# A job's output copied to SBUF by ScalarE, its sums and low parts formed on VectorE during the next job's value products

## The chip, the cores and the metric

The kernel runs on one core of a Trainium2 chip. A core has five engines with a queue of instructions each: TensorE (PE in the profile; its weight loads are shown apart as PEld), VectorE (DVE), ScalarE (ACT), GpSimd (POOL) and SyncE (SP), which here only issues DMAs. Each engine works through its own queue in order; semaphores hold an instruction until what it needs is there. The metric is the device time of one execution in microseconds (us); lower is better.

## The reference

What is computed, cut to what matters:

```python
# q, k, v: (2 batches, 8 heads, 576 positions, 64)
psi_rel = log1p(abs(i - j)); psi_i = log1p(max(i, 1))
bias    = relu((psi_rel / psi_i)[..., None] @ w1 + b1) @ w2        # 32 hidden units, 8 heads
attn    = softmax(q @ k.T / 8 + bias)                               # over 576 positions
x       = (attn @ v) laid out as (1152 tokens, 512)
x       = (silu(x @ w_gate) * (x @ w_val)) @ w_out                  # 512 -> 1536 -> 512
out     = softplus(x @ w_in) @ w_out2                               # 512 -> 2048 -> 512
```

All inputs are float32 (the weights of the two last lines float64).

## The kernel before

**Stages.** From 0 to about 60 us the position bias is computed. From there to about 188 us attention runs, and from 188 us to the end the two feed-forward layers, one long row of matmuls (lines 722, 673 and 1030).

**Units, jobs and slots.** Attention has eight units (a pair of heads of one batch each, in the order of `UNITS`, line 477). A unit has two jobs, `sub` 0 with 256 query rows per head and `sub` 1 with 320. I write job (4,1) for unit 4, sub 1. A job is cut into 4 or 5 chunks of scores, and `run_slot` (line 493) treats one chunk per slot, nine slots to a unit. The order in which a slot writes out its instructions is the order of every engine's queue in this stage (`manual_schedule` names all engines): scores on PE (`ps<-kst,ql` and `ps<-kst,qh`, line 326); `finish` of the job whose value products have just ended; copies of transposed blocks out of PSUM (`at<-pt`, mostly ACT, one piece on DVE); bias and row minimum on DVE (`e,sm<-ps,bias`, line 347); the exponential of the chunk before on ACT, its reciprocal on DVE and the scaling on POOL (line 369); two steps of preparing the next unit's keys and queries; the steps of jobs in `late`; transposes on PE (`pt<-ident,e`); and, in one slot of a job, all its value products on PE (`po<-at,v`, line 423) in one go.

**High and low parts.** An operand in float32 is split into a rounded high part and the rest (`kst`, `qh` and `ql`, `B11h` and `B11l`), so that three fast products give a precise one. Line 189 forms the rest for keys and queries, mostly on POOL, line 443 (the helper `minus`) for the outputs.

**What becomes of an output.** The first feed-forward layer is computed with seven products instead of eight: the output is cut into four quarters, units 0 and 2 giving B11, units 1 and 3 B12, units 4 and 5 B22, units 6 and 7 B21. Besides B11, B21 and B22 it wants the sums T1 = B12 - B11, T2 = B22 - T1, T3 = B22 - B12 and T4 = B21 - T2, each as high and low part. `finish` (line 433) forms all that from `po`, the one PSUM bank of value products. It is a generator: each `yield` hands the rest to the next slot. VectorE reads `po` two or three times in the slots that follow the job (`t2f<-po,bias`, `t<-po,bias`, `B22l<-po,B22h`); POOL forms the low parts of T2, T3 and mostly T4; ACT rounds the high parts.

**Buffers.** Two PSUM buffers hold scores (`psS`), three hold transposed blocks (`psT`), one holds `po`. A score can be written when the DVE instruction that read its buffer two scores earlier is done. `t` is one SBUF tile for T3 and T4 on their way to POOL.

Of the kernel before, what the change touches and what calls it, by code (L numbers as in the profile page):

```python
# [40 lines left out]
PLAIN = 2  # L41

WARM = 12


KHIGH, KLOW = "va", "ppvp"
# [54 lines left out]
def tile_kernel(ctx: ExitStack, tc, qT, kT, vS, vT, wb, wg, wv, wo, wi, wo2, table, out):  # L101
# [25 lines left out]
    with ExitStack() as actx:  # L127
# [303 lines left out]
        def finish(u):  # L431

            if u["i"] == 2 and u["sub"] == 0:
                slots(xp, "a", ("B21", "B22"))
            if u["i"] == 4 and u["sub"] == 0:
                right.close()
                SLOTS["rp8"] = (None, opener(rctx)("rp8", 1, side="right"))
                slots(SLOTS["rp8"][1], "r", ("T2", "T3", "T4"))
            pr, sub, po = u["pr"], u["sub"], u["po"]
            n = 320 if sub else 256  # L440
            cols = slice(256 * sub, 256 * sub + n)
            po = po[:, :n]
            minus = lambda o, a, b, eng=nc.vector: eng.tensor_tensor(o, a, b, op=ALU.subtract)
            at = lambda name: [t[:, pr % 2, cols] for t in SLOTS[name][1]]
            floats = lambda name: [t.bitcast(F32) for t in at(name)]
            name = f"B{1 + pr // 2}{1 + u['b']}"
            if name != "B12":
                nc.scalar.copy(at(name)[0], po)
            k = pr % 2
            home = bias[1][:, 2 * k : 2 * k + 2, cols]  # L450
            t1f, b12 = home[:, 0], home[:, 1]
            chains = []
            if name == "B12":
                nc.scalar.copy(b12, po)
                minus(t1f, po, floats("B11")[0])
                minus(t1f, t1f, floats("B11")[1])
                chains = [("T1", t1f)]
            elif name == "B22":
                t2, t3 = t2f[:, k, cols], tmpp.tile([P, 320], F32, name="t")[:, :n]
                minus(t2, po, t1f)  # L460
                minus(t3, po, b12)
                chains = [("T2", t2), ("T3", t3)]
            elif name == "B21":
                t4 = tmpp.tile([P, 320], F32, name="t")[:, :n]
                minus(t4, po, t2f[:, k, cols])
                chains = [("T4", t4)]
            if not u["eager"]:
                yield
            if name != "B12":
                minus(at(name)[1], po, floats(name)[0])  # L470
            if u["eager"]:
                yield
                yield
            for to, t in chains:
                nc.scalar.copy(at(to)[0], t)
                yield
                minus(at(to)[1], t, floats(to)[0], nc.vector if to == "T1" or u["eager"] else nc.gpsimd)

        UNITS = [(0, 0), (0, 1), (1, 0), (1, 1), (2, 1), (3, 1), (2, 0), (3, 0)]

# [8 lines left out]
        prep = iter(())  # L489
        before = None  # L490
        slot = 0

        def run_slot():
            nonlocal turned, done, prep, before, slot
# [28 lines left out]
                u = units[i][sub]  # L523
                got = scores(u, n)
            for w in done:
                w["eager"] = slot >= len(chunks) - 1
                late.append(finish(w))
                if w["eager"]:
                    next(late[-1])
# [7 lines left out]
                before = None  # L537
            for _ in range(2):
                next(prep, None)
            late[:] = [steps for steps in late if next(steps, late) is not late]  # L540
            held, turned = [t[:2] for t in turned], []

            over = slot >= len(chunks)
# [8 lines left out]
            for _ in range(len(gathered) if last_job else max(ends, default=0)):  # L552
                w, piece = gathered.pop(0)
                values(w, piece)
                if piece == PIECES[w["sub"]][-1]:
                    done.append(w)
            if slot < len(chunks):
                before = (u, n)
                if n == 3 + sub:
# [4 lines left out]
        with tc.manual_schedule(engines={E.PE, E.Activation, E.DVE, E.Pool, E.SP}):  # L564
# [26 lines left out]
            fp = pool("fp", 1)  # L591
            psT = pool("psT", 3, space=PSUM)
            psO = pool("psO", 1, space=PSUM)
            while slot < len(chunks) or jobs or turned or gathered or done or late:
                run_slot()


# [525 lines left out]
```

## Time and profile before

| | |
|---|---|
| median of 3 runs | 589.54 us (589.43 to 589.64) |
| the profiled execution's own time | 589.42 us |
| its span, first to last instruction | 587.6 us |
| PE busy | 579.3 us, 99% |
| PEld busy | 509.9 us, 87% |
| DVE busy | 452.9 us, 77% |
| ACT busy | 374.1 us, 64% |
| POOL busy | 98.9 us, 17% (nearly all of it between 50 and 181 us) |
| granted TensorE clock | 0.999 |

A busy PE in this table is not PE at its peak, since matmuls overlap and their ends are modelled. What PE loses in attention is better read from the weight loads (PEld): the idle time that a load shows in brackets, and what ended it.

### The profile page before, as it was taken

Reading aid. Unit: us, or ns where it says so; the run is one execution under the profiler, and the core shown is the slowest. Engines: PE = TensorE matmul, PEld = TensorE weight load, DVE = VectorE, ACT = ScalarE, POOL = GpSimd, SP = SyncE. Lnnn points to the kernel's source line nnn. Section 1 sums busy time; section 2 is a strip of 40 time slices with the busy share of each in tenths; the row PEclk is TensorE's granted clock in tenths of the full one; section 3 lists DMA queues with packets and bytes.
Section 4 is the critical chain, followed back from the end, with each engine's and each line's share of the span. In section 5 each row is a group of like instructions: output and inputs, shape, how many; then the busy total and the mean of one; then the engine's idle time right before and its main releaser. Section 6 shows DMA issues by size and latency. Waiting matters only on the chain.

```text
span 587.6 us, 11306 instructions
## 1 busy us (share of the span) xinstructions
PE 579.3 (99%) x4274; PEld 509.9 (87%) x4274; DVE 452.9 (77%) x972; ACT 374.1 (64%) x711; POOL 98.9 (17%) x147
## 2 busy tenths in 40 slices
PE   8999999999999999999999999999999999999997
PEld 6444578888887999999999999999989989989986
DVE  6999778788888998987879626579998876974432
ACT  6999887888888866755567425359736725733520
POOL 0002578888971000000000000000000000000000
PEclk9999999999999999999999999999999999999999
DMA  8999623333233342232344231222343241310012
GB/s 316 208 205 211 160 74 111 112 112 100 82 111 103 114 131 84 91 126 73 84 139 139 71 97 53 105 85 76 92 158 127 73 143 29 117 36 1 2 59 102
DMA packets 42038, 63.30 MB, mean 108 GB/s; under 512 B 4224, under 2 KB 30848, under 8 KB 41984
## 3 DMA queue, kind: packets, MB, share of 16 engines
q1 hardware_dynamic: 41840, 62.57, 36.4%
q8 instruction: 33, 0.54, 0.4%
q14 instruction: 21, 0.17, 0.1%
q10 hardware_dynamic: 144, 0.02, 0.0%
HBM read 49.60 MB, written 2.36 MB: 88 GB/s over the span
## 4 chain that ended last, share of the span: by engine, by line
PE 85%; DVE 7%; ACT 4%; POOL 2%; DMA 1%; issue 1%; POOLq 0%; DVEq 0%; ACTq 0%
PE pw L722 38%; PE pw L1030 17%; PE pw L673 13%; PE po L423 6%; PE ps L326 4%; PE pt L396 3%; PE pb L263 2%; ACT early L275 2%; ACT r L253 2%; DVE e L347 2%; PE ps L299 1%; DVE r L255 1%; DMA bias<-early 1%; PE warm L567 1%; DVE bias L347 1%
## 5 line engine op out<-in xcount | busy, mean ns | idle before, releaser
L1030 PE MATMUL pw<-oh,g2h 128*128 128x512 f32 x144 | 56.2, 390 | 0.0
L1030 PE MATMUL pw<-oh,g2l 128*128 128x512 f32 x144 | 56.2, 390 | 0.0
L1030 PE MATMUL pw<-ol,g2h 128*128 128x512 f32 x144 | 56.1, 390 | 0.0
L673 PE MATMUL pw<-gl,sh 128*128 128x384 f32 x144 | 48.2, 335 | 0.0
L673 PE MATMUL pw<-gh,sl 128*128 128x384 f32 x144 | 48.2, 334 | 0.0
L673 PE MATMUL pw<-gh,sh 128*128 128x384 f32 x144 | 48.2, 334 | 0.0
L255 DVE TENSOR_SCALAR r<-G 128x576 f32<-128x576 f32 x108 | 47.2, 514 | 0.0
L263 PE MATMUL pb<-r,wb_sb 128*32 128x288 f32 x576 | 46.7, 412 | 0.3 <-DVE r L255 0.2
L647 DVE SCALAR_TENSOR_TENSOR x<-raw,x 128x512 int32<-128x512 int32 x68 | 46.2, 687 | 0.9
L369 POOL TENSOR_SCALAR e<-e,sm 128x576 f32<-128x576 f32 x44 | 34.5, 795 | 66.3 <-DVE sm L366 58.9
L263 PEld LDWEIGHTS pb<-r,wb_sb 128*32 128x32 f32 x576 | 21.6, 109 | 24.4 <-DVE r L255 9.0
L347 DVE CUSTOM_DVE_ANT_0 e<-ps,bias 128x576 f32<-128x576 f32 x44 | 33.0, 749 | 12.4 <-PE ps L326 7.6
L403 ACT COPY at<-pt 128x512 f32<-128x512 f32 (+2 forms) x69 | 36.4, 547 | 6.0 <-PE pt L396 5.5
L326 PE MATMUL ps<-kst,ql 128*128 128x288 f32 x120 | 37.1, 338 | 1.4 <-DVE sm L347 0.7
L423 PE MATMUL po<-at,v 128*64 128x256 f32 (+3 forms) x384 | 36.8, 332 | 1.0 <-DVE at L403 0.8
L1068 DVE TENSOR_TENSOR acc<-pw,acc 128x512 f32<-128x512 f32 x27 | 17.5, 684 | 25.1 <-PE pw L1030 25.1
L361 ACT ACTIVATE e<-e,sm 128x576 f32<-128x576 f32 x44 | 34.3, 780 | 3.0 <-DVE sm L347 1.9
L644 DVE TENSOR_SCALAR x<-x 128x512 int32<-128x512 int32 x68 | 28.7, 427 | 9.3 <-ACT x L643 5.1
L423 PEld LDWEIGHTS po<-at,v 128*64 128x64 f32 x384 | 26.7, 137 | 8.2 <-issue 1.5
L1030 PEld LDWEIGHTS pw<-oh,g2l 128*128 128x128 f32 x144 | 27.0, 188 | 5.8
L326 PE MATMUL ps<-kst,qh 128*128 128x288 f32 x120 | 32.0, 295 | 0.0
L396 PE MATMUL pt<-ident,e 128*128 128x128 f32 x188 | 31.6, 276 | 0.1
(269 smaller groups left out, 1659.6 us busy)
## 6 DMA issues: line engine op xcount, KB each, us to landing
raw<-in_wo_dram SPq DMA_DIRECT2D x28, 512.0 KB, 3.5
bias<-early SPq DMA_DIRECT2D x32, 288.0 KB, 7.2
raw<-in_wi_dram SPq DMA_DIRECT2D x16, 512.0 KB, 4.0
raw<-in_wv_dram SPq DMA_DIRECT2D x12, 512.0 KB, 4.5
raw<-in_wg_dram SPq DMA_DIRECT2D x12, 512.0 KB, 3.6
qr<-in_qT_dram SPq DMA_DIRECT2D x7, 576.0 KB, 3.7
bias<-in_kT_dram SPq DMA_DIRECT2D x6, 576.0 KB, 4.4
v<-in_vS_dram SPq DMA_DIRECT2D x8, 384.0 KB, 3.3
```

Source lines behind the costliest of these rows:

```text
L255: nc.vector.tensor_scalar(r, G[:, w0 : w0 + S], PB[:, n : n + 1], 0.0, op0=ALU.add, op1=ALU.max)
L263: nc.tensor.matmul(pb[32 * ct : 32 * ct + 32, hf, :HALF], W2, rs[ct][:, HALF * hf : HALF * (hf + 1)], start=True, stop=True,)
L326: nc.tensor.matmul(ps[:, hf, :HALF], u[t][:, o : o + P], kst[:, a, HALF * hf : HALF * (hf + 1)], start=i == 0, stop=i == len(parts) - 1,)
L347: nc.vector.tensor_tensor_reduce(out=e[:, :S].rearrange("p (a n) -> p a n", a=2), in0=ps[:, :, :HALF], in1=bt.rearrange("p (a n) -> p a n" ...
L369: nc.gpsimd.tensor_scalar(e, e, sm[:, 3, i : i + 1], 1.0, op0=ALU.mult, op1=ALU.mult)
L396: nc.tensor.transpose(pt[:, P * w : P * (w + 1)], e, ident)
L403: marks[eng, u["i"], u["sub"]] = copy(at[:, :w], pt[:, :w]).ins
L423: nc.tensor.matmul(u["po"][D * a : D * (a + 1), o : o + n], v[:, D * t : D * (t + 1)], at[:, i : i + n], start=piece == 0 and o == 0, stop ...
L647: nc.vector.scalar_tensor_tensor(yi, lw, 29, yi, op0=ALU.logical_shift_right, op1=ALU.bitwise_or)
L673: nc.tensor.matmul(ps[:, :n], w[:, k], x, start=first and k == 0 and i == 0, stop=last and k == NK - 1 and i == 2)
L722: nc.tensor.matmul(ps[:, hf, :HALF], a[:, o + k], b[:, HALF * hf : HALF * (hf + 1)], start=start and k == 0 and i == 0, stop=k == 1 and i ...
L1030: nc.tensor.matmul(ps, g, w.rearrange("p k f -> p (k f)"), start=f == 0 and i == 0, stop=f == 3 and i == 2)
```

## The change

ACT now copies the output of a B22 or B21 job from `po` to SBUF at once (into `t` for sub 1; for sub 0 into `over`, the spare last columns of `bias4`). The subtractions then take the SBUF copy in place of `po`. The generator says `BLOCK` where it has to wait for the next job's value products: `advance` puts it into the list `waiting`, and `run_slot` goes on with that list right behind a job's value products. B11 is as before, B12's sum T1 and its low part wait in the same way, and the last job (7,1) still reads `po`.

```diff
+            over = bias[4][:, :2].rearrange("p a s -> p (a s)")[:, 5 * P :]
+            room = lambda: (tmpp.tile([P, 320], F32, name="t") if sub else over)[:, :n]
             if name == "B12":
                 nc.scalar.copy(b12, po)
-                minus(t1f, po, floats("B11")[0])
+                yield BLOCK
+                minus(t1f, b12, floats("B11")[0])
                 minus(t1f, t1f, floats("B11")[1])
-                chains = [("T1", t1f)]
-            elif name == "B22":
-                t2, t3 = t2f[:, k, cols], tmpp.tile([P, 320], F32, name="t")[:, :n]
-                minus(t2, po, t1f)
-                minus(t3, po, b12)
-                chains = [("T2", t2), ("T3", t3)]
-            elif name == "B21":
-                t4 = tmpp.tile([P, 320], F32, name="t")[:, :n]
-                minus(t4, po, t2f[:, k, cols])
-                chains = [("T4", t4)]
-            if not u["eager"]:
                 yield
-            if name != "B12":
+                nc.scalar.copy(at("T1")[0], t1f)
+                yield BLOCK
+                minus(at("T1")[1], t1f, floats("T1")[0])
+                return
...
+            t = room()
+            if u["i"] == 2 * NP - 1 and sub:
+                minus(t, po, t2f[:, k, cols])
+                minus(at(name)[1], po, floats(name)[0])
                 yield
+            else:
+                nc.scalar.copy(t, po)
+                yield BLOCK if u["i"] < 7 else None
+                minus(at(name)[1], t, floats(name)[0])
+                if name == "B22":
+                    minus(t2f[:, k, cols], t, t1f)
+                    chains = [("T2", t2f[:, k, cols])]
+                minus(t, t, b12 if name == "B22" else t2f[:, k, cols])
                 yield
+            chains.append(("T3" if name == "B22" else "T4", t))
             for to, t in chains:
                 nc.scalar.copy(at(to)[0], t)
                 yield
-                minus(at(to)[1], t, floats(to)[0], nc.vector if to == "T1" or u["eager"] else nc.gpsimd)
+                minus(at(to)[1], t, floats(to)[0], nc.vector if u["eager"] else nc.gpsimd)
...
-                w["eager"] = slot >= len(chunks) - 1
+                w["eager"] = slot >= len(chunks)
...
-            late[:] = [steps for steps in late if next(steps, late) is not late]
+            advance(late)
...
+            if done:
+                advance(waiting)
```

PE's and SP's queues are word for word the same; what moves stands on DVE, ACT and POOL.

**DVE, from the end of job (4,0) to the end of job (4,1).** Before (`bias_85` is the tile with the mixed chunk, `bias_83` and `bias_84` hold chunks, `bias_72` the next keys, `bias_73` b12 and t1f):

```order
L443 TENSOR_TENSOR t2f<-po,bias_73 128x256
L443 TENSOR_TENSOR t<-po,bias_73 128x256
L347 ISA bias_83,sm<-ps,bias_83 128x576
...
L185 CAST kst<-bias_72 128x576
L443 TENSOR_TENSOR B22l<-po,B22h 128x256
L347 ISA bias_83,sm<-ps,bias_83 128x576
...
L185 CAST qh<-qr 128x256
L347 ISA bias_84,sm<-ps,bias_84 128x576
```

After, the same stretch ends so, with the value products of (4,1) on PE beside it:

```order
L349 ISA bias_84,sm<-ps,bias_84 128x576
L349 ISA sm 128x1
L187 CAST qh<-qr 128x256
L445 TENSOR_TENSOR T1l<-bias_73,T1h 128x320
L445 TENSOR_TENSOR B22l<-bias_85,B22h 128x256
L445 TENSOR_TENSOR t2f<-bias_85,bias_73 128x256
L445 TENSOR_TENSOR bias_85<-bias_85,bias_73 128x256
L349 ISA bias_84,sm<-ps,bias_84 128x576
```

The three subtractions of (4,0) have left the places between its next chunks and stand, with a fourth that is left from (3,1), in one piece ahead of the first chunk behind the value products; none of them reads `po` any more.

**POOL, while unit 5 prepares its sub 1 and the keys of the unit after.** Before:

```order
L189 TENSOR_TENSOR ql<-qr,qh 128x320
L443 TENSOR_TENSOR T2l<-t2f,T2h 128x320
L443 TENSOR_TENSOR T3l<-t,T3h 128x320
L369 TENSOR_SCALAR e_104<-e_104,sm 128x576
L369 TENSOR_SCALAR e_105<-e_105,sm 128x576 x2
L189 TENSOR_TENSOR kst<-bias_72,kst 64x288 x3
L443 TENSOR_TENSOR T2l<-t2f,T2h 128x256
L369 TENSOR_SCALAR bias_83<-bias_83,sm 128x576 x2
L189 TENSOR_TENSOR ql<-qr,qh 128x256
L443 TENSOR_TENSOR T3l<-t,T3h 128x256
L189 TENSOR_TENSOR ql<-qr,qh 128x256
```

After:

```order
L445 TENSOR_TENSOR T2l<-t2f,T2h 128x256
L371 TENSOR_SCALAR e_104<-e_104,sm 128x576
L191 TENSOR_TENSOR ql<-qr,qh 128x320
L445 TENSOR_TENSOR T3l<-bias_85,T3h 128x256
L371 TENSOR_SCALAR e_104<-e_104,sm 128x576
L371 TENSOR_SCALAR e_105<-e_105,sm 128x576 x2
L191 TENSOR_TENSOR kst<-bias_72,kst 64x288 x2
L445 TENSOR_TENSOR T2l<-t2f,T2h 128x320
L191 TENSOR_TENSOR kst<-bias_72,kst 64x288
L445 TENSOR_TENSOR T3l<-t,T3h 128x320
L371 TENSOR_SCALAR bias_83<-bias_83,sm 128x576 x2
L191 TENSOR_TENSOR ql<-qr,qh 128x256 x2
```

T3l no longer stands between the two 256-wide `ql`; the low parts of one job now come about one job later, T2l ahead of the second 320-wide `ql` and among the keys.

**ACT, around the end of job (5,0).** Before:

```order
L448 CAST B22h<-po 128x256
L403 COPY at<-pt 128x512
L361 ACTIVATE e_105,sm<-e_105,sm 128x576
L475 CAST T2h<-t2f 128x256
L403 COPY at<-pt 128x512 x2
```

After:

```order
L487 CAST T2h<-t2f 128x320
L450 CAST B22h<-po 128x256
L477 COPY bias_85<-po 128x256
L405 COPY at<-pt 128x512
L363 ACTIVATE e_105,sm<-e_105,sm 128x576
L487 CAST T3h<-t 128x320
L405 COPY at<-pt 128x512 x2
```

One copy is added, and it writes where POOL's T3l of the job (4,0) still reads, so it waits for POOL; T2h, now of the job before, stands ahead of it.

## Rows read from the trace of the kernel before

**Rows 1.** Timeline, PEld, 78 to 130 us: start, us, instruction, idle before and releaser.
```profile
78.43 0.19 PEld L326 LDWEIGHTS ps<-kst,ql 128*128 128x128 f32 x1 [0.34 <-POOL ql L189]
80.62 0.19 PEld L326 LDWEIGHTS ps<-kst,ql 128*128 128x128 f32 x1 [0.32 <-DVE sm L347]
...
89.89 0.19 PEld L326 LDWEIGHTS ps<-kst,ql 128*128 128x128 f32 x1 [0.30 <-DVE sm L347]
...
94.08 0.19 PEld L326 LDWEIGHTS ps<-kst,ql 128*128 128x128 f32 x1 [0.39 <-issue]
...
97.96 0.19 PEld L326 LDWEIGHTS ps<-kst,ql 128*128 128x128 f32 x1 [0.73 <-DVE sm L347]
...
120.95 0.30 PEld L326 LDWEIGHTS ps<-kst,ql 128*128 128x128 f32 x2 [0.43 <-DVE sm L347]
...
128.40 0.19 PEld L326 LDWEIGHTS ps<-kst,ql 128*128 128x128 f32 x1 [0.36 <-POOL ql L189]
```

**Rows 2.** Timeline, PEld, 142 to 172 us.
```profile
145.63 0.19 PEld L326 LDWEIGHTS ps<-kst,ql 128*128 128x128 f32 x1 [0.40 <-POOL ql L189]
...
146.63 0.19 PEld L326 LDWEIGHTS ps<-kst,ql 128*128 128x128 f32 x1 [0.20 <-DVE sm L347]
...
153.76 0.30 PEld L326 LDWEIGHTS ps<-kst,ql 128*128 128x128 f32 x2 [0.29 <-DVE sm L347]
...
155.39 0.19 PEld L326 LDWEIGHTS ps<-kst,ql 128*128 128x128 f32 x1 [0.21 <-DVE sm L347]
...
162.29 0.19 PEld L326 LDWEIGHTS ps<-kst,ql 128*128 128x128 f32 x1 [0.31 <-POOL ql L189]
...
163.28 0.19 PEld L326 LDWEIGHTS ps<-kst,ql 128*128 128x128 f32 x1 [0.21 <-DVE sm L347]
...
170.40 0.30 PEld L326 LDWEIGHTS ps<-kst,ql 128*128 128x128 f32 x2 [0.28 <-DVE sm L347]
```

**Rows 3.** Timeline, PE, in the last jobs.
```profile
180.53 0.65 PE L423 MATMUL po<-at,v 128*64 128x256 f32 x4 [0.77 <-DVE at L403]
```

**Rows 4.** Two stretches: length, busy us of each engine, clock, DMA share, GB/s.
```profile
150.00:160.00 10.00, 9.95 (x92) 8.80 (x91) 8.06 (x24) 8.59 (x21) 9.33 (x13) 1.00 0.19 61
190.00:200.00 10.00, 10.00 (x78) 10.00 (x77) 8.98 (x21) 9.05 (x16) 0.00 (x0) 1.00 0.49 151
```

**Rows 5.** Line 443: count, ns min/median/max, first and last start, shapes.
```profile
L443 DVE TENSOR_TENSOR T1l<-bias,T1h x4: 404/552/908, 79.5 to 132.5; 128x256 fp32r<-128x256 f32 x2, 128x320 fp32r<-128x320 f32 x2
L443 DVE TENSOR_TENSOR t2f<-po,bias x4: 402/436/470, 135.5 to 161.7; 128x256 f32<-128x256 f32 x2, 128x320 f32<-128x320 f32 x2
```

**Rows 6.** Timeline, DVE and POOL, 122 to 125 us.
```profile
122.22 2.83 POOL L189 TENSOR_TENSOR kst<-bias,kst 64x288 fp32r<-64x288 f32 x3
...
123.00 0.46 DVE L189 TENSOR_TENSOR kst<-bias,kst 64x288 fp32r<-64x288 f32 x1 [0.81 <-ACT kst L183]
123.48 0.91 DVE L443 TENSOR_TENSOR T1l<-bias,T1h 128x256 fp32r<-128x256 f32 x1
```

**Rows 7.** Timeline, DVE, behind the value products of (4,1), (5,0) and (5,1).
```profile
140.89 0.70 DVE L365 TENSOR_SCALAR sm<-sm 128x2 f32<-128x2 f32 x1
...
143.63 0.76 DVE L347 CUSTOM_DVE_ANT_0 bias<-ps,bias 128x576 f32<-128x576 f32 x1 [0.75 <-PE ps L326]
...
150.93 0.76 DVE L347 CUSTOM_DVE_ANT_0 e<-ps,bias 128x576 f32<-128x576 f32 x1 [1.12 <-PE ps L326]
...
160.42 0.76 DVE L347 CUSTOM_DVE_ANT_0 bias<-ps,bias 128x576 f32<-128x576 f32 x1 [0.88 <-PE ps L326]
```

**Rows 8.** Timeline, POOL, 140 to 153 us.
```profile
140.84 0.73 POOL L443 TENSOR_TENSOR T2l<-t2f,T2h 128x256 fp32r<-128x256 f32 x1
...
144.15 0.74 POOL L443 TENSOR_TENSOR T3l<-t,T3h 128x256 fp32r<-128x256 f32 x1
...
151.69 0.89 POOL L443 TENSOR_TENSOR T3l<-t,T3h 128x320 fp32r<-128x320 f32 x1
```

**Rows 9.** Timeline, ACT, behind the value products of (5,0).
```profile
150.93 0.36 ACT L448 CAST B22h<-po 128x256 fp32r<-128x256 f32 x1
```

More of the change, by code (lines that the diff above doesn't have):

```diff
@@ L43 @@
 WARM = 12
+BLOCK = "block"
 KHIGH, KLOW = "va", "ppvp"
@@ L452, in finish @@
             chains = []
+            over = bias[4][:, :2].rearrange("p a s -> p (a s)")[:, 5 * P :]
+            room = lambda: (tmpp.tile([P, 320], F32, name="t") if sub else over)[:, :n]
             if name == "B12":
                 nc.scalar.copy(b12, po)
-                minus(t1f, po, floats("B11")[0])
+                yield BLOCK
+                minus(t1f, b12, floats("B11")[0])
                 minus(t1f, t1f, floats("B11")[1])
-                chains = [("T1", t1f)]
-            elif name == "B22":
-                t2, t3 = t2f[:, k, cols], tmpp.tile([P, 320], F32, name="t")[:, :n]
-                minus(t2, po, t1f)
-                minus(t3, po, b12)
-                chains = [("T2", t2), ("T3", t3)]
-            elif name == "B21":
-                t4 = tmpp.tile([P, 320], F32, name="t")[:, :n]
-                minus(t4, po, t2f[:, k, cols])
-                chains = [("T4", t4)]
-            if not u["eager"]:
-                yield
-            if name != "B12":
-                minus(at(name)[1], po, floats(name)[0])
-            if u["eager"]:
-                yield
+                yield
+                nc.scalar.copy(at("T1")[0], t1f)
+                yield BLOCK
+                minus(at("T1")[1], t1f, floats("T1")[0])
+                return
+            if name == "B11":
+                yield
+                minus(at(name)[1], po, floats(name)[0])
+                return
+            t = room()
+            if u["i"] == 2 * NP - 1 and sub:
+                minus(t, po, t2f[:, k, cols])
+                minus(at(name)[1], po, floats(name)[0])
+                yield
+            else:
[6 more added lines that the diff above has]
+                minus(t, t, b12 if name == "B22" else t2f[:, k, cols])
                 yield
+            chains.append(("T3" if name == "B22" else "T4", t))
             for to, t in chains:
@@ L491, in tile_kernel, with advance @@
         slot = 0
+        waiting, ended = [], object()
+        def advance(which):
+            steps_now, which[:] = which[:], []
+            for steps in steps_now:
+                said = next(steps, ended)
+                if said is BLOCK:
+                    waiting.append(steps)
+                elif said is None:
+                    late.append(steps)
         def run_slot():
@@ L593, in tile_kernel @@
             psO = pool("psO", 1, space=PSUM)
-            while slot < len(chunks) or jobs or turned or gathered or done or late:
+            while slot < len(chunks) or jobs or turned or gathered or done or late or waiting:
                 run_slot()
```

## The prediction

> **What bounds the kernel now.** I read the busy times by stretch first. From 190 us on PE is busy in every microsecond [rows 4], and the chain of waits runs through PE alone there; so whatever attention gains or loses arrives at the end whole. Inside attention PE looks busy too (9.95 of 10 us), but beside it POOL has 9.33, ACT 8.59 and DVE 8.06 [rows 4]: four engines near their limit, each feeding the others. What PE really loses is read next, from the weight loads ahead of the scores. Each load behind a value product shows 0.38 or 0.39 us of idle whichever engine is named, as at 94.08 [rows 1]; that is a pattern of its own, and I leave it out. What remains are six waits before 130 us (0.34 + 0.32 + 0.30 + 0.73 + 0.43 + 0.36 = 2.48 us [rows 1]), seven after it (0.40 + 0.20 + 0.29 + 0.21 + 0.31 + 0.21 + 0.28 = 1.90 us [rows 2]) and 0.77 us in the last jobs [rows 3]. That is 5.15 us, 0.9% of the kernel, and all that a change in attention can win. Nine of the thirteen name DVE's bias step and four POOL's `ql`; hence the third view, who stands ahead of those two on DVE and POOL.
>
> **The change part by part.** All sums go against the profiled execution's 589.42 us (587.6 us of span and 1.8 us around it); the median, 589.54, lies 0.12 above, and I add that at the end.
>
> *Waits that go.* The waits of 97.96, 120.95, 146.63, 153.76, 155.39, 163.28 and 170.40 each have one or two subtractions of line 443 just ahead of the bias step that PE waits for; that of 80.62 has T1l. These leave for the value products. 128.40 waits for a `ql` that is late because DVE spent 0.91 us on T1l [rows 6] ahead of it; 145.63 and 162.29 wait for a `ql` that has T3l (0.74 us [rows 8]) in front of it, which moves. 89.89 stands behind B11's low part, which stays, and 78.43 behind POOL's scaling: of its 0.34 I take 0.10. So before 130 us: 0.10 + 0.32 + 0.73 + 0.43 + 0.36 = 1.94 us; after: 1.90 us. What is late next are the copies and exponentials on ACT; the wait at 97.96 may keep half of its 0.73, since ACT's T1h now waits for the moved pair. In the last jobs the pair of subtractions (up to 0.47 us each [rows 5]) goes from ahead of the last bias step, but a copy and a waiting T4h join ACT: of 0.77 us [rows 3] I take 0.5, with 0 and 0.77 as bounds.
>
> *The added copies.* Seven copies out of PSUM on ACT, by the cast beside them 0.36 us for 256 columns [rows 9], by its width some 0.45 for 320: 2.8 us. They stand where ACT copies transposed blocks, of which PSUM holds three; T2h and T3h leave the same stretch at about the same price. I cost them at nothing; without that cover 0.36 us at a job's end, four to seven times, 1.4 to 2.5 us.
>
> *The subtractions in their new place.* The bias step behind the value products waits for PE's scores: 0.75, 1.12, 0.88 us of idle DVE [rows 7]. But 256 columns from PSUM cost 0.40 to 0.47 us whatever POOL does, while the same subtraction from SBUF costs 0.404 to 0.908 [rows 5], and the moved ones are now all of the second kind. Rows 6 show why: POOL is in three operations without a pause, DVE does one subtraction in 0.46 us, and the next, ready at once, takes 0.91, because a POOL operation went between. If they take turns like that, n subtractions cost n times 0.41 to 0.47 and a POOL operation of 0.73 to 0.89 us [rows 8] between any two, with about 0.4 for the one in progress.
>
> The Trainium skill ("SBUF — State Buffer", section "Who interferes with whom") says that a DVE instruction with two SBUF inputs contends with a GpSimd instruction that reads SBUF, one with at most one SBUF input does not, and that the loser blocks for the whole instruction. By that rule the trace agrees (0.470 at most against 0.908); if it did not hold, the sum below would lose its last term.
>
> What a place can hide: DVE's idle time, plus what the bias step may slip until PE needs its PSUM buffer two scores on. That slip is 145.63 - 0.40 - (143.63 + 0.76) = 0.84 us at (4,1) [rows 2, 7] and 162.29 - 0.31 - (160.42 + 0.76) = 0.80 at (5,1); for (5,0) and (6,0) I take 0.8 from these two.
> - (4,1): four subtractions, 0.47 + 3 x 0.41 = 1.70, and 0.4 + 2 x 0.74 for POOL, which then has nothing more ready: 3.6 us. Room 0.75 + 0.84 + 0.5 (the step of 0.70 us at 140.89 [rows 7] falls into T2l [rows 8], which leaves): 2.1. Over by 1.5.
> - (5,1): three, 1.23 + 0.4 + 2 x 0.74 = 3.1; room 0.88 + 0.80 = 1.7, since ACT's keys decide when DVE gets there. Over by 1.4.
> - (5,0) and (6,0): 3 x 0.47 + 0.4 + 2 x 0.89 = 3.6; room 1.12 + 0.8 and the 1.4 us of three subtractions that left: 3.3. Over by 0.3 each.
> - The places before have one to three subtractions and the room of T1l besides: nothing.
>
> That is 3.5 us if they always take turns, 0 if DVE keeps the port from one to the next. The pair of rows 6 takes turns, and I found no pair that does not; I take 3.3, near the upper end, for a turn now and then that finds POOL idle (0.67 of 10 us [rows 4]).
>
> Sum: -1.94 - 1.90 - 0.5 + 3.3 = -1.04 us, 588.4 in the profiled execution, 588.5 us as a median. Gain and price are both three to four times as large as what is left.
>
> **The rivals.**
> - *The cover is enough.* DVE runs its three or four in one piece, at most 0.4 us of waiting ahead: 1.6 to 2.1 us, which each room holds. For it: idle and slack are there in every place. Against it: rows 6. It gives -1.94 - 1.90 - 0.5 = -4.3; POOL, held 13 times for at most 0.41 us, has 0.67 of every 10 us free [rows 4], 2.3 in the 35 us that count, and could lose 5.3 - 2.3 = 3.0 us, of which a third is as much as PE would see: 585.2 to 586.2 us.
> - *Slower: POOL becomes the bound from (5,0) to (6,0).* A unit lasts 162.29 - 145.63 = 16.66 us there [rows 2], of which POOL is busy 93% [rows 4], some 15.5. Six subtractions that hold it for their whole 0.41 to 0.47 us add 2.6: 18.1, 1.5 us over, in two units. T2l now stands ahead of the second `ql`, and ACT's new copy may not overwrite `over` before T3l has read it: in the old trace a T3l ends at 152.58 [rows 8], the copy would stand at 151.29 [rows 9], and behind it the copies that PE needs: up to 1.3 us more. It decides from the point where the next unit's `ql` comes later than PE's scores by more than the 1.9 us won there. Price: 588.5 + 3.0 = 591.5, less if the stalls fall together: about 591. The rule of the Trainium skill ("SBUF — State Buffer", section "Who interferes with whom"), taken at its word, is this mechanism at its dearest. For it: POOL has next to no pauses; against it: T2l and T3l only moved, and PE's stalls give POOL time to catch up.
> - *Nothing comes of it.* The chain from scores over exponential, keys and `ql` to the next unit's scores runs over ACT; if that sets the unit's length, the stalls only change their names: 589.5 us.
>
> **How the numbers follow.** My forecast has 0.44, the cover 0.28, POOL as the bound 0.20, nothing 0.08. The predicted time is 588.5 us. The forecast's own range is 587.4 to 589.7; reaching into the first rival down to 585.4 and into the second up to 590.9 leaves about 2 in 10 out. A measurement of this kernel tells some 0.2% from no change, 1.2 us: below 588.36 is faster, above 590.72 slower. The forecast gives 0.22 to faster, 0.21 to same and 0.01 to slower; the first rival 0.28 to faster; the second 0.19 to slower and 0.01 to same; the third 0.08 to same. Together 0.50, 0.30, 0.20.
>
> **What would show it.** In the profile after: the waits before 130 us at 97.96, 120.95 and 128.40 are gone or small, and PE's first feed-forward matmul comes 1 to 2 us earlier than at 188. Taking turns shows as moved subtractions of 0.7 us and more with a POOL operation between, and as new PE waits for DVE's bias step two scores behind the value products of (4,1) and (5,1). If those subtractions stand 0.35 us apart, the first rival holds. If PE waits for `ql` at the start of units 6 and 7 by a microsecond, or ACT's copy names POOL's T3l, it is the second. I am wrong altogether if attention's length changes without a change in these PE waits, or if the feed-forward part gets PE waits of its own.

## The result and the profile after

The changed kernel takes 595.44 us (median of 4 runs, 595.24 to 596.30) against 589.52 (4 runs): ratio 1.0103, 95% interval 1.0086 to 1.0121. It is slower by 5.9 us, the other way from the forecast and outside the range. The profiled execution, the longest of the four, has a span of 594.3 us against 587.6. Times without a unit are in us.

Where the time went is read first from the start of each job's value products on TensorE:

| start of | before | after | after minus before |
|---|---|---|---|
| (2,0) | 99.13 | 98.04 | -1.09 |
| (4,0) | 131.39 | 129.68 | -1.71 |
| (4,1) | 139.75 | 138.58 | -1.17 |
| (5,0) | 147.79 | 148.32 | +0.53 |
| (6,0) | 164.44 | 168.30 | +3.86 |
| (6,1) | 172.95 | 177.31 | +4.36 |
| first feed-forward product | 188.12 | 193.69 | +5.57 |

Up to 130 us the change gives what was forecast. Between 130 and 194 us it loses 7.3. The weight loads with waits that answer to [rows 1] are down to these, beside those of 0.38 or 0.39 and a few of 0.3 or less elsewhere:

```profile
89.55 0.19 PEld L328 LDWEIGHTS ps<-kst,ql 128*128 128x128 f32 x1 [0.31 <-DVE sm L349]
...
105.38 0.19 PEld L328 LDWEIGHTS ps<-kst,ql 128*128 128x128 f32 x1 [0.28 <-DVE sm L349]
```

The matmuls that waited from 140 us on, in the kernel after (start, duration, instruction, idle before it and releaser). They answer to [rows 2, 3]:

```profile
144.09 0.40 PE L328 MATMUL ps<-kst,ql 128*128 128x288 f32 x1 [0.71 <-POOL ql L191]
146.02 0.37 PE L328 MATMUL ps<-kst,ql 128*128 128x288 f32 x1 [0.69 <-DVE sm L367]
154.28 0.66 PE L398 MATMUL pt<-ident,bias 128*128 128x128 f32 x4 [0.48 <-ACT at L405]
160.78 0.76 PE L425 MATMUL po<-at,v 128*64 128x128 f32 x5 [0.78 <-DVE at L405]
164.66 0.40 PE L328 MATMUL ps<-kst,ql 128*128 128x288 f32 x1 [0.65 <-POOL ql L191]
167.82 0.33 PE L398 MATMUL pt<-ident,bias 128*128 128x128 f32 x1 [0.36 <-POOL bias L371]
174.26 0.66 PE L398 MATMUL pt<-ident,bias 128*128 128x128 f32 x4 [0.47 <-ACT at L405]
...
185.31 0.65 PE L425 MATMUL po<-at,v 128*64 128x256 f32 x4 [1.08 <-DVE at L405]
189.10 1.29 PE L425 MATMUL po<-at,v 128*64 128x320 f32 x12 [0.81 <-ACT at L405]
196.11 0.50 PE L770 MATMUL pw<-B11h,wh 128*128 128x288 f32 x2 [0.57 <-DVE B21l L445]
```

They sum to 6.6 us, where PE before had 0.77 [rows 3] and two of 0.3 or less, and they name DVE, ACT and POOL: no single wait took the place of the old ones. What they have in common is seen in the row of subtractions behind (4,1)'s value products. The timeline of DVE, then of POOL, at the same time:

```profile
142.18 0.48 DVE L445 TENSOR_TENSOR T1l<-bias,T1h 128x320 fp32r<-128x320 f32 x1
142.57 0.88 DVE L445 TENSOR_TENSOR B22l<-bias,B22h 128x256 fp32r<-128x256 f32 x1
143.38 0.94 DVE L445 TENSOR_TENSOR t2f<-bias,bias 128x256 f32<-128x256 f32 x1
144.35 0.84 DVE L445 TENSOR_TENSOR bias<-bias,bias 128x256 f32<-128x256 f32 x1
145.12 0.74 DVE L349 CUSTOM_DVE_ANT_0 bias<-ps,bias 128x576 f32<-128x576 f32 x1
...
141.37 1.82 POOL L371 TENSOR_SCALAR bias<-bias,sm 128x576 f32<-128x576 f32 x2 [1.35 <-PE po L425]
143.16 1.76 POOL L191 TENSOR_TENSOR ql<-qr,qh 128x256 fp32r<-128x256 f32 x2
```

Four subtractions take 3.0 us here where they could take 1.8 (number 6 below), and the bias step behind them comes without DVE having idled (in [rows 7] it had 0.75). POOL pays as well: its two `ql` of 256 columns take 0.88 and 0.91 here, and one took 0.74 in the trace of before. The next unit shows how such lateness goes round. Rows of four engines, in order of time:

```profile
152.60 0.73 POOL L445 TENSOR_TENSOR T3l<-bias,T3h 128x256 fp32r<-128x256 f32 x1
...
153.37 0.37 ACT L477 COPY bias<-po 128x256 f32<-128x256 f32 x1 [1.37 <-POOL T3l L445]
...
155.02 0.15 DVE L367 TENSOR_SCALAR sm<-sm 128x1 f32<-128x1 f32 x1 [1.49 <-ACT e L363]
...
155.54 0.81 POOL L371 TENSOR_SCALAR e<-e,sm 128x576 f32<-128x576 f32 x1 [0.76 <-DVE sm L368]
...
157.67 2.33 DVE L191 TENSOR_TENSOR kst<-bias,kst 64x288 fp32r<-64x288 f32 x1 [1.26 <-ACT kst L185]
158.06 0.86 POOL L445 TENSOR_TENSOR T2l<-t2f,T2h 128x320 fp32r<-128x320 f32 x1
...
158.90 0.78 POOL L191 TENSOR_TENSOR kst<-bias,kst 64x288 fp32r<-64x288 f32 x1
...
160.03 0.69 DVE L405 COPY at<-pt 128x512 f32<-128x512 f32 x1
...
161.55 0.78 ACT L363 ACTIVATE m<-m,sm 128x576 f32<-128x576 f32 x1 [2.78 <-DVE sm L349]
```

ACT's new copy waits 1.37 us for POOL's T3l (the kernel before has no such copy), the exponential behind it is late, DVE waits 1.49 for that, POOL 0.76 for DVE. Then DVE's subtraction for the keys, which the change does not move, stands 2.33 us beside POOL's row (0.46 in [rows 6]); the copy behind it is what PE waits 0.78 us for at 160.78. Two stretches, 150 to 160 and 190 to 200 us, and the unit from (5,0) to (6,0):

```profile
150.00:160.00 10.00, 9.47 (x79) 7.53 (x75) 7.14 (x17) 7.40 (x20) 9.08 (x12) 1.00 0.19 61
190.00:200.00 10.00, 9.43 (x81) 8.20 (x77) 9.06 (x20) 7.66 (x16) 0.00 (x0) 1.00 0.32 93
...
148.32:168.30 19.98, 17.68 (x142) 14.05 (x141) 16.51 (x44) 15.00 (x39) 16.98 (x23) 1.00 0.17 53
```

Against [rows 4] DVE and ACT do less in ten microseconds while POOL is as busy as before, and the unit lasts 19.98 us instead of 16.65 (164.44 - 147.79; POOL was busy 15.50 of these).

### The profile page after: what moved, and what is told of

It reads as the page before. It is cut to its first block, busy times and chain, and to the rows that moved or that the text cites. A ratio compares the mean times of both kernels' runs of the same rounds, so it can differ in the third digit from the quotient of the medians.

```text
span 594.3 us, 11296 instructions
## 1 busy us (share of the span) xinstructions
PE 581.3 (98%) x4274; PEld 509.8 (86%) x4274; DVE 461.2 (78%) x971; ACT 375.1 (63%) x718; POOL 104.0 (17%) x148
## 4 chain that ended last, share of the span: by engine, by line
PE 77%; DVE 9%; ACT 8%; POOL 2%; DMA 1%; issue 1%; DVEq 0%; ACTq 0%; POOLq 0%
PE pw L748 37%; PE pw L1056 17%; PE pw L699 13%; PE po L425 3%; PE pt L398 2%; ACT early L277 2%; ACT r L255 2%; PE pb L265 2%; PE ps L328 2%; PE ps L301 1%; ACT at L405 1%; DVE r L257 1%; DMA bias<-early 1%; PE warm L593 1%; DVE e L349 1%
## 5 line engine op out<-in xcount | busy, mean ns | idle before, releaser
L371 POOL TENSOR_SCALAR e<-e,sm 128x576 f32<-128x576 f32 x44 | 35.8, 824 | 64.8 <-DVE sm L368 60.3
L425 PE MATMUL po<-at,v 128*64 128x256 f32 (+3 forms) x384 | 38.0, 333 | 2.7 <-DVE at L405 1.9
```

The costliest lines, as they stand in the source:

```text
L371: nc.gpsimd.tensor_scalar(e, e, sm[:, 3, i : i + 1], 1.0, op0=ALU.mult, op1=ALU.mult)
L425: nc.tensor.matmul(u["po"][D * a : D * (a + 1), o : o + n], v[:, D * t : D * (t + 1)], at[:, i : i + n], start=piece == 0 and o == 0, stop ...
```

## The experiments

The texts on record speak of these theories. A: the loss is made by subtractions with both operands in SBUF and POOL's instructions holding each other up. B: it begins with the B12 part. C: it is ACT's copy waiting for T3l. D: the last jobs lose by themselves. E: it is the new order and place. Ratios are to the kernel before on the same chip, with 95% intervals; differences in us are of medians, and the kernel before had 589.5 to 590.1 on these chips, so they are good to about half a microsecond.

**1. B12 alone.** The branches for B22 and B21, and the rule for the last jobs, are those of the kernel before.

> Only the B12 part of the change (jobs (2,0) to (3,1): copy to SBUF, sums and T1l where the next job's value products stand); B22 and B21 as in the kernel before. The first term of my sum was -1.9 for this, and the changed kernel is 1.7 us ahead at 129.68. Theory A (the loss is made by the moved B22 and B21 subtractions between 130 and 194 us, which take turns with POOL): 587.5 to 588.3. Theory B (the loss begins with B12, whose T1h copies on ScalarE now wait up to 2.2 us for VectorE and push what stands behind them): 589.3 or more.

589.80, ratio 1.0003 (0.9994 to 1.0012): inside B's range and not A's. But it is no slower than the kernel before either, so the 5.9 us come only with B22 and B21. It is 1.83 us ahead at (4,0), 1.09 at (4,1), and 0.13 behind at (5,0). So the B12 part does not make the loss, but its gain does not live either. The keys' subtraction of one unit earlier pays, beside three of POOL's (0.46 in the kernel before):

```profile
138.18 1.70 DVE L191 TENSOR_TENSOR kst<-bias,kst 64x288 fp32r<-64x288 f32 x1 [0.74 <-ACT kst L185]
```

**2. Two places for the copy.**
```diff
-            room = lambda: (tmpp.tile([P, 320], F32, name="t") if sub else over)[:, :n]
+            room = lambda: (tmpp.tile([P, 320], F32, name="t") if sub else over[:, 256 * (u["i"] % 2) :])[:, :n]
```


> The changed kernel, but the 256-column jobs copy their output by turns to two places instead of one, so that ScalarE's copies for (5,0) and (6,0) need not wait (1.37 us each) until POOL has read the place as T3. All else as in the changed kernel. Theory C (that wait, with the gather copies behind it, is most of the loss): 2.5 to 4 us less than the changed kernel, 591.5 to 593. Theory A (taking turns of VectorE and POOL): at most 1 us less, 594.4 to 595.5.

593.90, ratio 1.0066 (1.0049 to 1.0083). 1.5 us less than the changed kernel, between what C and A expected: without the wait a quarter of the loss is gone. That is more than the wait alone: in the profiled execution the keys' subtraction, now at 156.33, takes 0.71 instead of 2.33, and PE waits 1.25 us for `ql` at 162.62 and 1.35 for DVE at 165.21 instead.

**3. T2l to T4l on DVE.**
```diff
-                minus(at(to)[1], t, floats(to)[0], nc.vector if u["eager"] else nc.gpsimd)
+                minus(at(to)[1], t, floats(to)[0], nc.vector)
```


> The changed kernel, but the subtractions T2l, T3l and T4l run on VectorE, none on POOL, which keeps its key, query and scaling work. Theory A (POOL and VectorE in each other's way): POOL's seven low parts (0.5 to 0.9 us each) no longer stand in a row with the keys' subtraction, so VectorE's 2.33 us subtraction at 157.67 falls to about 1 us; VectorE gets some 5 us more work of its own, spread over 60 us: 593 to 594.5. Theory C (ScalarE waits for POOL's T3l): about the same, as T3l comes earlier on VectorE or not. If VectorE's own load is the bound: 597 or more.

592.44, ratio 1.0043 (1.0028 to 1.0058): 3.0 us less, more than A expected. The keys' subtraction that took 2.33 us takes 0.60. More work on DVE made the kernel faster; what stands on POOL counts.

**4. B21 as before.** The branch of the kernel before stands in for the four jobs from (6,0) on (with T4 of sub 0 in `over`).

> The changed kernel for B12 and B22; the four B21 jobs (6,0) to (7,1) as in the kernel before (the output read where it was accumulated, right after the copy; the rule for the last jobs as before). Theory D (the last jobs lose by themselves: VectorE's subtractions against POOL's scaling, copies on ScalarE, T4l on POOL): the 1.7 us between the start of (6,0)'s value products and the first product of the output projection come back, 593.2 to 594. Theory A: a little more, since (6,0)'s own subtractions no longer stand against POOL, 592.7 to 593.7. If the tail's loss was only carried over from before it: 595 to 595.5.

592.87, ratio 1.0049 (1.0034 to 1.0064), 2.6 us less: in A's range, below D's. From (6,0) to the first feed-forward product it needs 23.9 us, the changed kernel 25.4, the kernel before 23.7. So the last jobs lose 1.5 to 1.7 us by themselves. Behind that product the changed kernel loses 0.9 more against this run (400.6 us to the end of the span, and 399.7). What stands there in the changed kernel:

```profile
183.84 1.10 POOL L371 TENSOR_SCALAR bias<-bias,sm 128x576 f32<-128x576 f32 x1 [3.79 <-DVE sm L368]
...
185.17 0.82 DVE L445 TENSOR_TENSOR B21l<-t,B21h 128x320 fp32r<-128x320 f32 x1
...
187.83 0.37 ACT L477 COPY bias<-po 128x256 f32<-128x256 f32 x1 [0.99 <-POOL T4l L445]
...
195.59 0.46 ACT L487 CAST T4h<-t 128x320 fp32r<-128x320 f32 x1 [1.18 <-DVE t L445]
```

**5 and 6. POOL's work cut to an eighth, before and after.** In both kernels alike:
```diff
+            if by == "p" and i > 2:
+                l, h, src = (x[:, : x.shape[-1] // 8] for x in (l, h, src))
...
+                        e = e[:, : S // 8] if u["i"] > 2 else e
                         nc.gpsimd.tensor_scalar(e, e, sm[:, 3, i : i + 1], 1.0, op0=ALU.mult, op1=ALU.mult)
...
-                minus(at(to)[1], t, floats(to)[0], nc.vector if u["eager"] else nc.gpsimd)
+                c = n if to == "T1" or u["eager"] else n // 8
+                minus(at(to)[1][:, :c], t[:, :c], floats(to)[0][:, :c], nc.vector if u["eager"] else nc.gpsimd)
```


> The kernel before, with POOL's work of jobs 3 to 7 cut to an eighth of its columns: the lower parts of keys and queries, T2l to T4l and the scaling of the exponentials keep their places and their waits, but write only the first eighth (TensorE reads qh in place of ql, and the upper parts of T2 to T4 in place of the lower, so the values are not the reference's). It is the base for the next run. All theories: the waits for POOL go and VectorE is never held, 586 to 589.

> The changed kernel with the same cut of POOL's work to an eighth (same things left out as in the run before it). Theory A (the changed kernel loses because its SBUF subtractions and POOL's instructions hold each other up): with POOL's instructions short the loss is gone, and the time is below that of the kernel before with the same cut, by 1 to 4 us. Theory E (the loss comes from the order: subtractions late, more copies on ScalarE, VectorE's row of four in the window; POOL's long instructions have little part in it): still 3 us or more above the kernel before with the same cut.

587.07 (0.9952, 0.9937 to 0.9967) without the change and 584.75 (0.9911, 0.9895 to 0.9928) with it. TensorE reads `qh` in place of `ql` in both, so its waits for POOL's `ql` go too. With POOL out of the way the change wins 2.3 us; with POOL whole it loses 5.9. E is out: the order is the same in both. The four subtractions that took 3.0 us, here grouped by line (count, ns min/median/max):

```profile
L448 DVE TENSOR_TENSOR T1l<-bias,T1h x1: 478/478/478, 140.1 to 140.1; 128x320 fp32r<-128x320 f32 x1
L448 DVE TENSOR_TENSOR B22l<-bias,B22h x1: 471/471/471, 140.5 to 140.5; 128x256 fp32r<-128x256 f32 x1
L448 DVE TENSOR_TENSOR t2f<-bias,bias x1: 417/417/417, 140.9 to 140.9; 128x256 f32<-128x256 f32 x1
L448 DVE TENSOR_TENSOR bias<-bias,bias x1: 424/424/424, 141.3 to 141.3; 128x256 f32<-128x256 f32 x1
```

But the cut takes two things away at once: the holding up, and POOL's own lateness (T3l, `ql`, the scaling), so it does not size A alone.

**7. Not moved, from SBUF.**
```diff
-                yield BLOCK if u["i"] < 7 else None
+                yield
```


> The changed kernel, but the subtractions of B22 and B21 don't wait for the next job's value products: they follow ScalarE's copy by one slot, about where the kernel before has them, and read the SBUF copy. B12 as in the changed kernel. Theory A (SBUF operands against POOL, wherever they stand): the loss stays, 594 to 597. Theory E (the place is at fault: in the window they stand in a row of three or four ahead of the gather's copies and the exponentials' sums): most of the loss goes, 589.5 to 591.5.

600.14, ratio 1.0170 (1.0155 to 1.0186), 3.1 past A's range (594 to 597) and far from E's: the place in the window was the better one. That the SBUF operands are the trouble fits, but this run does not single them out, since ACT's copies stay and the three subtractions stand in another order than in the kernel before. Here the row stands ahead of a bias step for which PE waits. Timeline of DVE and PE, and a stretch:

```profile
137.04 0.88 DVE L445 TENSOR_TENSOR t2f<-bias,bias 128x256 f32<-128x256 f32 x1
137.96 0.90 DVE L445 TENSOR_TENSOR bias<-bias,bias 128x256 f32<-128x256 f32 x1
138.78 0.74 DVE L349 CUSTOM_DVE_ANT_0 bias<-ps,bias 128x576 f32<-128x576 f32 x1
...
139.59 0.61 PE L328 MATMUL ps<-kst,ql 128*128 128x288 f32 x1 [2.22 <-DVE sm L349]
...
140.00:150.00 10.00, 10.00 (x86) 8.97 (x87) 7.17 (x22) 6.95 (x18) 7.26 (x10) 0.85 0.33 99
```

The last row adds that after this wait of 2.22 us the granted clock was 0.85 over the next ten microseconds, 1.2 instead of 2.4 GHz for a part of them; some of the 600 is that. The four executions had a mean granted clock of 0.990 to 0.997.

**8. Three mends together** (2, 3 and 4).

> The changed kernel with the three mends at once: two places for the 256-column copies, T2l to T4l on VectorE, B21 as in the kernel before. Alone they gave 1.5, 3.0 and 2.6 us off the changed kernel; if they add up, 588.3. If they take the same time twice: 590 to 592.

592.64, ratio 1.0046 (1.0031 to 1.0061): they do not add up, the three together are no better than number 3. At the start of (6,0) the two stand alike (166.22 and 166.23), so the second place gives nothing once T3l is off POOL; from there to the first feed-forward product they need 24.9 and 24.6 us, so B21's mend gives nothing on top either. That all three take the same lateness out of one circle is my reading of it.

**9 to 12. The operand in PSUM.** A second output buffer in PSUM is paid here with one of the three for transposes:
```diff
-            psT = pool("psT", 3, space=PSUM)
-            psO = pool("psO", 1, space=PSUM)
+            psT = pool("psT", 2, space=PSUM)
+            psO = pool("psO", 2, space=PSUM)
```


> The kernel before with two PSUM buffers for the jobs' outputs and two instead of three for the transposes (the eight banks are full). No subtraction moves. If TensorE's waits for the output's buffer (rows 1 and 2 of my prediction, 3.8 us) can be had without any SBUF copy and two transposes' buffers are enough: 585.7 to 588. If the third buffer of the transposes is needed: 590 or more.

598.38, ratio 1.0143 (1.0127 to 1.0159). PE then waits 8.3 us, in 16 places between 78 and 190 us, for a transposes' buffer that the gather's copies have not read yet. The third buffer is needed, and all four runs of this group bear that price.

> The changed kernel with the same two buffers for outputs and two for transposes, the subtractions still from the SBUF copy. It is the base for the next run; 593 to 597, or more if two transposes' buffers are too few.

601.66, ratio 1.0192 (1.0167 to 1.0217). Now only the first operand changes:
```diff
-                minus(t1f, b12, floats("B11")[0])
+                minus(t1f, po, floats("B11")[0])
...
-                minus(at(name)[1], t, floats(name)[0])
+                minus(at(name)[1], po, floats(name)[0])
...
-                    minus(t2f[:, k, cols], t, t1f)
+                    minus(t2f[:, k, cols], po, t1f)
...
-                minus(t, t, b12 if name == "B22" else t2f[:, k, cols])
+                minus(t, po, b12 if name == "B22" else t2f[:, k, cols])
```


> As the run before it, with ScalarE's copies and every instruction at its place, but the moved subtractions that took the SBUF copy as their first operand take the output itself, in PSUM (one operand in PSUM, one in SBUF). Theory A (two SBUF operands are what lets POOL and VectorE hold each other up): 3 to 7 us less than the run before it. Theory E (place and order): within 1 us of it.

599.09, ratio 1.0148 (1.0127 to 1.0168): 2.6 us less, just under A's 3 to 7 and well over E's 1. The intervals just touch, and the granted clock differed within each run. At a clock of 1.000 number 10 took 600.60 and number 11 597.49 (one execution each); at 0.996 and 0.997 number 10 took 602.48 and 602.54, number 11 599.04 to 599.23. That is 3.1 and 3.4 us, inside A's range. Against number 9, whose executions all had 1.000, the change at that clock costs 2.2 us with the SBUF operand and gains 0.9 with the operand in PSUM. The instructions say the same. First DVE and POOL with the SBUF operand, behind (4,1)'s value products:

```profile
146.92 0.88 DVE L445 TENSOR_TENSOR B22l<-bias,B22h 128x256 fp32r<-128x256 f32 x1
147.72 0.95 DVE L445 TENSOR_TENSOR t2f<-bias,bias 128x256 f32<-128x256 f32 x1
148.70 0.85 DVE L445 TENSOR_TENSOR bias<-bias,bias 128x256 f32<-128x256 f32 x1
...
147.50 1.77 POOL L191 TENSOR_TENSOR ql<-qr,qh 128x256 fp32r<-128x256 f32 x2
```

Then the same with the operand in PSUM:

```profile
146.52 0.41 DVE L445 TENSOR_TENSOR B22l<-po,B22h 128x256 fp32r<-128x256 f32 x1
146.85 0.41 DVE L445 TENSOR_TENSOR t2f<-po,bias 128x256 f32<-128x256 f32 x1
147.18 0.41 DVE L445 TENSOR_TENSOR bias<-po,bias 128x256 f32<-128x256 f32 x1
...
147.09 1.43 POOL L191 TENSOR_TENSOR ql<-qr,qh 128x256 fp32r<-128x256 f32 x2
```

Same place, same POOL work beside it: 2.7 us of DVE become 1.2, and POOL's two `ql` need 0.34 less. In the fourth run the copies go, which nothing reads any more:
```diff
-                nc.scalar.copy(t, po)
                 yield BLOCK if u["i"] < 7 else None
```


> As the run before it, without ScalarE's seven or so copies of B22 and B21 to SBUF, which nothing reads any more. Theory A: 0 to 1 us less than the run before it, since ScalarE is not the bound. Theory C (ScalarE's copies that wait for POOL's T3l): 1.5 us less or better.

597.09, ratio 1.0120 (1.0104 to 1.0136). By the medians this is 2.0 us less, C's number and not A's. But C is not shown by it. All four executions here had a granted clock of 1.000; the single one of number 11 that had it too took 597.49, 0.4 more, which is A's number. And the profiled execution of number 11 (0.997) loses its time not at ACT's copy, which waits 0.61 us there, but at the keys' subtraction. DVE, POOL and PE in number 11, then DVE and POOL here:

```profile
160.47 2.65 DVE L191 TENSOR_TENSOR kst<-bias,kst 64x288 fp32r<-64x288 f32 x1 [0.93 <-ACT kst L185]
160.44 0.80 POOL L191 TENSOR_TENSOR kst<-bias,kst 64x288 fp32r<-64x288 f32 x1
163.89 0.66 PE L398 MATMUL pt<-ident,e 128*128 128x128 f32 x4 [2.65 <-DVE at L405]
...
160.53 0.46 DVE L191 TENSOR_TENSOR kst<-bias,kst 64x288 fp32r<-64x288 f32 x1 [0.86 <-ACT kst L185]
160.57 1.07 POOL L191 TENSOR_TENSOR kst<-bias,kst 64x288 fp32r<-64x288 f32 x1
```

DVE's subtraction started 0.03 us behind POOL's there and took 2.65; here it started 0.04 ahead of it and took 0.46, and POOL's took 1.07. After the wait of 2.65 us on PE the granted clock was 0.57 from 165 to 169 us in number 11, 1.2 GHz for most of it. This run is also 1.3 us below number 9, though the intervals overlap: moved, with operands in PSUM and without the copies, the subtractions seem to win.

**13 and 14. Which of POOL's work.** Numbers 6's cut without its edit of the scaling, and with that edit alone.

> The changed kernel with POOL's subtractions of jobs 3 to 7 cut to an eighth of their columns (lower parts of keys and queries, T2l to T4l; same things left out as in the two runs with POOL's work cut) but the scaling of the exponentials whole. If the scaling alone holds the moved subtractions up enough to make the loss: 590 or more. If the subtractions of POOL do: near the run with all of POOL's work cut, 585 to 587.

> The counterpart: the changed kernel with the scaling alone cut to an eighth of its columns for jobs 3 to 7 (so the probabilities are mostly unscaled), POOL's subtractions whole. If the scaling makes the loss: 585 to 588. If POOL's subtractions do: 591 or more. If either kind is enough while POOL stays busy with the other: both runs lie between, 587 to 591.

587.07 (0.9959, 0.9945 to 0.9973) with POOL's subtractions cut, 592.20 (1.0040, 1.0027 to 1.0054) with the scaling cut. The first is 8.4 us below the changed kernel, the second 3.2, about where both were expected if POOL's subtractions make the loss (the first is 0.07 outside). The scaling has a smaller part. The kernel before was not run with either cut alone; number 5, with both, took 587.07 as well.

**15 and 16. T2l to T4l on DVE, without the change and with B12 alone** (number 3's edit).

> The kernel before with T2l to T4l on VectorE instead of POOL: the counterpart of the run in which this took 3.0 us off the changed kernel. Theory A (the gain there is the end of POOL's row of keys and low parts against the moved subtractions): here, with operands in PSUM, it gains nothing or costs VectorE's time, 589 to 592. If it gains 3 us here too, that step has nothing to do with the change: 586.5.

588.83, ratio 0.9985 (0.9975 to 0.9994), 0.2 below A's range and far from 586.5. It gains 0.8 us here and 3.0 in the changed kernel, so most of number 3's gain belongs to the change. It is the one version that leaves nothing out and is clearly below both kernels, by little.

> Only the B12 part of the change, with T2l to T4l on VectorE. The B12 part alone was 1.8 us ahead at 129.6 us and gave it back by 148 us, 1.2 us of it where VectorE's subtraction for the keys took 1.70 us beside three of POOL's in a row. If the rest of the change is worth having without POOL in the way: 588 to 589, less than both kernels. If VectorE's own load takes the gain instead: 590 to 592.

589.20, ratio 0.9994 (0.9985 to 1.0003), between the two expectations: B12's part adds nothing to number 15.

**17 and 18. The keys' lower parts all on POOL,** on top of 16 and 15.
```diff
-KHIGH, KLOW = "va", "ppvp"
+KHIGH, KLOW = "va", "pppp"
```


> The B12 part alone with T2l to T4l on VectorE (589.2), and with the fourth of the keys' lower parts on POOL too, so that VectorE has no subtraction beside three of POOL's keys. If that subtraction (0.93 us in the trace at 138.2) is what takes the early gain of 1.8 us between 129 and 148 us: 588 to 588.7, below the kernel before with the same two swaps. If POOL's four in a row come too late for the keys, or VectorE's load takes the gain: 589.5 to 591.

> The kernel before with T2l to T4l on VectorE (588.83) and the fourth of the keys' lower parts on POOL. Base for the run before it. VectorE's subtraction for the keys took 0.46 to 0.71 us here, POOL's about 0.8, so a change of at most half a microsecond: 588.3 to 589.3.

590.40 (1.0008, 0.9999 to 1.0017) with B12's part, in the second of my ranges, and 592.74 (1.0047, 1.0034 to 1.0059) without. My range for the run without ended 3.4 us lower: with four in a row on POOL, PE waits 3.6 us for bias steps in five places (0.7 in two in number 15). With that, B12's part is worth 2.3 us. So its gain shows where PE waits for DVE anyway, and not in the kernel as it is. Which wait eats it there, the keys' subtraction or DVE's load as a whole, these two runs did not settle.

## Why the prediction was wrong

**The step that failed is the third term, the subtractions in their new place, +3.3 us: it let only the moved subtractions pay for POOL, each place by itself.** That POOL and DVE hold each other up is shown: numbers 11 and 10 differ in the operand alone, and 0.41 us stands against 0.85 to 0.95. But the moved rows themselves came out below my working: 3.0, 1.8, 2.1 and 1.8 us behind the value products of (4,1) to (6,0) (DVE, from 142.18, 150.08, 162.80 and 170.06 on), 8.7 together, where I had 3.6, 3.6, 3.1 and 3.6. The loss came out far above it. With POOL's work short the change is worth -2.3 us, with it whole +5.9: 8.2 us (ACT's copies and the last jobs included) for what I priced at 3.3. Only (4,1) paid as I had it: from there to (5,0) the loss is 1.70 us, and I had 1.5. What was not in my sum:
- I let each place pay by itself and pass on what was over its room. But POOL's lateness holds ACT's copy, that the exponentials, those DVE, and DVE the keys, on which POOL's next row stands. The unit from (5,0) to (6,0), for which I had 0.3 us at (5,0) and 1.4 at (5,1), got 3.3 us longer.
- The keys' subtraction, which does not move, pays too: 1.10 us at 138.3 and 2.33 at 157.67 in the changed kernel, where it took 0.46 and 0.75 before.
- "The places before: nothing" does not hold for (3,1): its first subtraction, at 132.0, took 1.16 us (0.47 before).

The Trainium skill ("SBUF — State Buffer", section "Who interferes with whom") says that at most one SBUF input, outside DVE's 2-port modes, keeps a DVE instruction clear of GpSimd, and that whoever has the shared ports holds them for the whole instruction. The traces agree: 0.41 us with POOL busy throughout in number 11, and 2.33 us in the changed kernel. They add a case: DVE's subtraction of 157.67 had started, by its record, before POOL's T2l did at 158.06, and still T2l and a keys' subtraction of POOL went ahead of it. My "a turn each" was too kind there. In all traces that have it from 100 us on, the keys' subtraction on DVE took 1.70 to 2.65 us in six places (the changed kernel and numbers 1, 4, 10, 11 and 14), and each time it had started inside an instruction of POOL behind which two more followed without a gap. Where POOL was idle, a gap of 0.07 or 0.08 followed, or at most one more instruction before a longer pause, it took 0.45 to 1.10.

**Waits before 130 us, -1.94:** right, -1.71 at (4,0). Those of [rows 1] at 97.96, 120.95 and 128.40 are gone.

**Waits from 142 to 172 us, -1.90:** not seen. Even with POOL's work cut, the change gains only 0.8 us between (4,0) and the first feed-forward product (54.99 to 54.21), though in that base some of these waits are gone already.

**The last jobs, -0.5:** wrong in sign. They lose 1.5 to 1.7 us (number 4). And a sign came that I had named for being wrong altogether: the feed-forward part has a PE wait of its own, 0.57 us at 196.11 for B21l of the last job. Of the 6.7 us by which the profiled span is longer, 1.1 lie behind the first feed-forward product.

**ACT's copies at nothing:** wrong. Number 2 puts 1.5 us on the wait of two of them for T3l, inside the bounds of 1.4 to 2.5 that I gave for lost cover, but by a wait that I had only in the rival. Number 12 adds 0.4 at like clock.

**The rivals.** The cover was not enough. The second, slower, is the one that came, with the signs I named for it: `ql` late at 144.09 and 164.66, though by 0.71 and 0.65 us and not the microsecond that I named, and ACT's copy naming T3l. But its reason is not quite right. POOL is busy 16.98 of 19.98 us in that unit, 85%, less than the 93% of [rows 4]: its busy time is 1.48 us above the 15.50 of before, where the rival had 2.6; it is not full, it is held up and then waited for, and it waits itself (0.76 at 155.54). The unit took 19.98 us where the rival had 18.1, and its 591 was 4.4 us short. I gave it 0.20, though [rows 6] spoke for it, because I set a gain and a price of the same size against each other as if the price could not feed on itself.

What stays open: how the 8.2 us divide between the holding up itself and POOL's lateness. The PSUM operand alone gave 2.6 us by the medians, 3.1 to 3.4 at like clock, in kernels that were short of a transposes' buffer; number 13 says that it is POOL's subtractions above all.

## What to carry to other kernels

Before moving a subtraction's operand from PSUM to SBUF, look at what GpSimd does beside it: with one operand in PSUM 256 columns cost 0.41 us, with both in SBUF up to 0.95, and GpSimd's own instruction grows too (0.74 to 0.91). Where engines that are busy 81 to 93% [rows 4] feed each other, a lateness is not used up at its place; price it by the loop, or test it by cutting one engine's work short in both kernels, which here turned a loss of 5.9 us into a gain of 2.3. A copy into a single buffer waits for that buffer's last reader (1.37 us here), and everything behind the copy on its engine waits too. And before a difference of 2 us is given to an edit, compare executions with the same granted clock: in number 12 that left 0.4 of 2.0.

## What the runs showed that I had not expected

- A subtraction of 0.46 us on DVE can take 2.33 or 2.65, with POOL's next instructions going ahead of it; in numbers 11 and 12 the two starts, relative to POOL's, lie 0.07 us apart.
- Giving the third buffer for transposes to the output costs 8.4 us net (598.38 against 590.00 on the same chip).
- Moving work from POOL to a DVE that is 71 to 81% busy between 150 and 160 us made both kernels faster, by 0.8 and 3.0 us.
